# Longformer attention with a mixer behind it: two row groups for the global tokens' products, and the second token layer's last rows for two batches at once

## The chip, the cores and the metric

The kernel runs on one core of one Trainium2 chip. The metric is the time of one execution on the device, in microseconds, as the median of several runs. Beside the timed runs there is one execution under the hardware profiler; every row of a profile below comes from that one. In its rows PE is TensorE (PEld its weight loads), DVE is VectorE, ACT is ScalarE, POOL is GpSimd, and SP is the engine that issues most DMAs; a q behind an engine's name is its sequencer. L595 is line 595 of the kernel.

## The reference

Eight batches of eight heads, 576 tokens, 64 values a head. Attention sees a band of 32 tokens to each side, and eight global tokens, which see all and are seen by all. Its output, 576 x 512 for a batch, goes through a mixer: a token layer over the 576 tokens and a channel layer over the 512 channels, each with a relu in the middle and a residual.

```python
mask = |i - j| <= 32  or  i is global  or  j is global
attn = softmax(where(mask, q @ k.T / 8, -1e9))
x = (attn @ v)                                  # (8, 576, 512), heads side by side
h = relu(x.T @ w_tok1) @ w_tok2                 # w_tok1 (576, 256), w_tok2 (256, 576)
u = x + h.T
out = u + relu(u @ w_ch1) @ w_ch2               # w_ch1 (512, 1536), w_ch2 (1536, 512)
```

## The kernel before

**Tiling.** The 576 tokens are four tiles of 128 and a last one of 64. Matrix products take 16-bit floats and add up in 32-bit in TensorE's output memory, from which VectorE or ScalarE fetch the results. Three pools hold these outputs: `psS`, three buffers of two times 512 columns, for attention and the token layers; `psM`, two of 512 columns, for the channel layers.

**Steps of a batch.** `S_` computes transposed scores of a pair of heads, each head on 64 of the array's 128 rows (`r = slice(64 * par, 64 * par + 64)`), ScalarE takes their exponentials into `e_all`, and `SM` masks them. `GK` computes the scores of the global keys, for four pairs of heads in four groups of 32 output rows, and gives `lf`: on row 32 p + 16 r + g stands head 2 p + r, and g counts eight global keys (the other eight rows of the sixteen are masked). `OG` sums the values that belong to these rows; its result, multiplied with a block pattern `blk`, is `rf`. `PV` (from L576) makes one tile of 128 tokens of x: for each head two products of 66 columns from the band (L586, L591; the last tile has one), and then for each half of four heads one product of `lf` with `rf` over all 128 rows and 264 columns (L595), which adds the global keys. VectorE divides by the sums and writes the tile into `x16s` (L602, L603).

**Token layers.** `M1` multiplies a tile of x with `w1` (two products of 512 columns for each tile, L618); after the fifth tile the relu gives `a1`. The fifth tile has 64 tokens. An even batch keeps them on rows 0 to 63 of its tile, an odd batch on rows 64 to 127; the weights for it, `w1l`, exist in two copies with the other rows at zero. `M2(b, part)` is the second token layer: parts 0 and 1 make two tiles of 128 tokens each (four products of 512 columns, L642, with adds on VectorE, L648), part 2 the last 64 tokens (two products and an add on 64 rows, L651). An even and the following odd batch share one tile `ul` for these, so that the channel layers of the last rows (`M4l`, the last `M5`) run once for two batches. `M3` transposes u by DMA on SP's queue, for the channel layers. Batch 0 has versions of its own (`M23_first`, `M3_first`), where TensorE transposes.

**Channel layers.** `M4` (twelve steps of four products, L697, with a relu on ScalarE, L703) and `M5` (eight steps of six products, L726, with an add and a store) are independent of the next batch's attention. They stand in a list, `dense`.

**Order.** The order of each engine's queue is written by hand: an instruction stands in the queue of its engine in the order in which the program calls it. `period(b)` runs the dense list of batch b between the attention steps of batch n = b + 1; `d(k)` takes the next k entries. In the same period the loads, casts and transposes of q and k for batch n + 1 and beyond are called (m = b + 2). `casts(b, engine)` lists nine casts of one batch: the rest rows first, then q and k of each pair of heads. For batch 3 the period n = 2 calls three of them on ScalarE behind `scores(0, ..)`, two behind `scores(1, ..)`, and the last three on Pool, then issues batch 4's loads on Pool (`load(4)`) and batch 3's transposes on SP (`turns(3)`).

**Loads.** Ahead of batch 0's value products Pool issues the weights, mixed with casts of v (`castv`): `w1`; then both copies of `w1l` and `w2` (`load_wt`, L223); then the channel weights, the gathers of the global tokens, and half of batch 1's q and k. SP loads the first batches' q, k and v and, later, those of batch 3.

Of the kernel before, what the change touches and what calls it, by code (L numbers as in the profile page):

```python
# [26 lines left out]
def kernel(  # L27
# [142 lines left out]
    idx_i = const.tile([P, 4], I32)  # L170
    gpm = const.tile([P, 1], F32)
    hb = const.tile([P, 1], F32)
    blk = const.tile([P, H], F32)

    def positions():
        nc.vector.tensor_mul(out=sel, in0=sel, in1=gidx_f)
# [36 lines left out]

    w1 = const.tile([P, NT - 1, DTOK], F16)
    w1l = const.tile([P, 2, DTOK], F16)
    w2 = const.tile([P, 2, NT * P], F16)
    wc1 = const.tile([P, 4, DCH], F16)
    wc2 = const.tile([P, NJ, DM], F16)

    def load_w1():  # L220
        nc.gpsimd.dma_start(out=w1, in_=moe_w_tok1[0 : S - LAST, :].rearrange("(c p) x -> p c x", p=P))

    def load_wt():  # L223
        nc.gpsimd.dma_start(out=w1l[0:LAST, 0], in_=moe_w_tok1[S - LAST : S, :])
        nc.gpsimd.dma_start(out=w1l[LAST:P, 1], in_=moe_w_tok1[S - LAST : S, :])
        nc.gpsimd.dma_start(out=w2[:, :, 0:S], in_=moe_w_tok2.rearrange("(c p) x -> p c x", p=P))

    def load_wc1(h0):
        nc.gpsimd.dma_start(
# [17 lines left out]
    nc.gpsimd.memset(kgz, 0.0)  # L247

    eg = const.tile([P, NT, H, GW], F16)
    x16s = [const.tile([P, NT, DM], F16, name=f"x16_{i}") for i in range(2)]  # L250

    def w_pads():
        nc.gpsimd.memset(w1l, 0.0)
        nc.gpsimd.memset(w2[:, :, S:], 0.0)

    def pads(i, eng):
        eng.memset(vsh[i][0:WIN, 0], 0.0)
        eng.memset(vsh[i][P - WIN : P, NT - 1], 0.0)
        eng.memset(vsh[i][:, :, :, D + 1 : VW], 0.0)
        eng.memset(vsh[i][:, :, :, D : D + 1], 1.0)  # L260
        eng.memset(x16s[i][LAST - 64 * i : P - 64 * i, NT - 1, :], 0.0)

    far = const.tile([P, NT, EW - 64], F16)
    bandm = const.tile([P, NT, EW - 64], F16)
# [295 lines left out]
    def OG(b):  # L560
        s = st[b]
        ps = pss([P, 2, VW], name=f"og_{b}")
        for c in range(NT):
            for p in range(NP):
                nc.tensor.matmul(  # L565
                    ps[32 * p : 32 * p + 32], lhsT=eg[:, c, 2 * p : 2 * p + 2, :],
                    rhs=vsh[b % 2][:, c, 2 * p : 2 * p + 2, :], start=(c == 0), stop=(c == NT - 1),
                )
        rf = mb.tile([P, NP, 2, VW], F16, tag="rf", name=f"rf_{b}")
        nc.vector.tensor_tensor(  # L570
            out=rf, in0=ps.unsqueeze(1).to_broadcast([P, NP, 2, VW]),
            in1=blk.rearrange("p (n r) -> p n r", r=2).unsqueeze(3).to_broadcast([P, NP, 2, VW]), op=ALU.mult,
        )
        s["rf"] = rf

    def PV(b, tau):  # L576
        s = st[b]

        odd_last = tau == NT - 1 and b % 2 == 1
        sh = 64 if odd_last else 0  # L580
        ps = pss([P, 2, 512], name=f"pv_{b}_{tau}")
        for hf in range(2):
            for hh in range(NP):
                h = NP * hf + hh
                o = ps[:, hf, VW * hh : VW * hh + VW]
                nc.tensor.matmul(  # L586
                    o, lhsT=e_all[:, h, tau, EW - P - sh : EW - sh], rhs=vsh[b % 2][:, tau, h, :],
                    start=hh == 0, stop=False,
                )
                if tau < NT - 1:  # L590
                    nc.tensor.matmul(  # L591
                        o, lhsT=e_all[:, h, tau + 1, 0:P], rhs=vsh[b % 2][:, tau + 1, h, :], start=False, stop=False
                    )
        for hf in range(2):
            nc.tensor.matmul(  # L595
                ps[:, hf, 0 : NP * VW], lhsT=s["lf"][:, P * tau - sh : P * tau - sh + P],
                rhs=s["rf"][:, 2 * hf : 2 * hf + 2], start=False, stop=True,
            )
# [4 lines left out]
        nc.vector.tensor_tensor(  # L603
            out=x16s[b % 2][r, tau, :].rearrange("p (f h x) -> p f h x", f=2, h=NP), in0=pq[r, :, :, 0:D],
            in1=rr[r].unsqueeze(3).to_broadcast([P if tau < NT - 1 else 64, 2, NP, D]), op=ALU.mult,
        )

    def M1(b, ch):
        s = st[b]
        if ch == 0 and b == 0:  # L610
            s["a1p"] = [psm([P, 512], name=f"a1p_{b}_{tt}") for tt in range(2)]
        elif ch == 0:
            ps = pss([P, 2, 512], name=f"a1p_{b}")
            s["a1p"], s["a1pp"] = [ps[:, 0], ps[:, 1]], ps
        ps = s["a1p"]
        for tt in range(2):
            w = w1[:, ch, P * tt : P * tt + P] if ch < NT - 1 else w1l[:, b % 2, P * tt : P * tt + P]
            nc.tensor.matmul(ps[tt], lhsT=w, rhs=x16s[b % 2][:, ch, :], start=(ch == 0), stop=(ch == NT - 1))  # L618
# [10 lines left out]
        if b % 2 == 0:  # L629
            s["ul"] = mb.tile([P, DM], F16, tag="ul", name=f"ul_{b}")  # L630
        else:
            s["ul"] = st[b - 1]["ul"]

    def M2(b, part):
        s = st[b]
        x16 = x16s[b % 2]
        taus = ((0, 1), (2, 3), (4,))[part]
        ps = pss([P, 2, 512], name=f"hp_{b}_{part}")
        sh = 64 if (part == 2 and b % 2) else 0
        for i, tau in enumerate(taus):  # L640
            for ch in range(2):
                nc.tensor.matmul(  # L642
                    ps[:, i, :], lhsT=w2[:, ch, P * tau - sh : P * tau - sh + P], rhs=s["a1"][:, ch, :],
                    start=(ch == 0), stop=(ch == 1),
                )
        if part < 2:
            for i, tau in enumerate(taus):
                nc.vector.tensor_add(out=s["u16"][:, tau], in0=x16[:, tau], in1=ps[:, i])  # L648
        else:
            r = slice(sh, sh + 64)  # L650
# [104 lines left out]
    def period(b):  # L755
# [30 lines left out]
        if n == 1:  # L786
            d(1)
            gather_t(0)
            globals_(1)
            T(1, 1)  # L790
            TE_q(1, 1, act)
            TE_k(1, 1, dve)
            masks_d()
            pads(1, nc.vector)
            d(1)
# [173 lines left out]
    load_wc1(8)  # L969
    load_wc2(0)  # L970
    load_wc2(4)
    GK(0)
    OG(0)
    lf_mask(0, 384)
# [61 lines left out]
```

## Time and profile before

| | us |
|---|---|
| three timed runs: median | 313.42 |
| lowest and highest | 313.31 to 315.36 |
| profiled execution | 313.69 |
| its span, from the first to the last instruction | 311.9 |

The granted clock of TensorE was 0.997 of the full one over the span. The chain that ended last, followed back from the last instruction, lies on TensorE for 82% of the span and on DMAs for 7%; 29% are the second channel layer (L726), 25% the first (L697). In lists by line a row reads: line, engine, operation, what it writes and reads, sizes, count, then busy time and the mean of one. In timelines the first column is the start in us from the beginning of the span, the second the time from the first start to the last end of the instructions in that row; what stands in brackets is idle time ahead of them, and what ended it.

### The profile page before, as it was taken

The numbers are of one execution on the slowest core, as the hardware profiler recorded it, in microseconds if no ns is written. First come the engines' busy times: TensorE is split into PE (matmuls) and PEld (weight loads), VectorE is DVE, ScalarE is ACT, GpSimd is POOL, SyncE is SP. The second block draws the span as 40 slices with busy tenths as digits, with TensorE's granted clock in tenths as the row PEclk, the third lists the DMA queues.
The fourth block names the chain that finished last, engine by engine and source line by source line (L and its number), as shares of the span: only waits on it lengthen the run. The fifth ranks groups of instructions, "written<-read, shape, count | busy, mean of one in ns | idle before, by whom it ended". The sixth has DMA issues, their size and how long they took to land.

```text
span 311.9 us, 6688 instructions
## 1 busy us (share of the span) xinstructions
PE 297.4 (95%) x2672; PEld 158.4 (51%) x2672; DVE 193.1 (62%) x429; ACT 164.2 (53%) x289; POOL 75.0 (24%) x118
## 2 busy tenths in 40 slices
PE   8987989997999999999999999999999999999993
PEld 7563545453465445544574445544574446444641
DVE  7985797575655677577854577577744585530021
ACT  5864773466739465576548473676443283206500
POOL 8785960496622002300230003200000000000000
PEclk9999999999999999999999999999999999999998
DMA  6999999899999999948995699954602410051022
GB/s 195 234 250 223 224 181 286 234 244 193 241 202 155 176 358 143 106 84 260 261 129 55 164 355 119 98 124 139 95 20 50 138 49 2 12 138 71 0 103 67
DMA packets 108513, 48.19 MB, mean 154 GB/s; under 512 B 87106, under 2 KB 102338, under 8 KB 108482
## 3 DMA queue, kind: packets, MB, share of 16 engines
q1 hardware_dynamic: 69712, 33.83, 48.3%
q0 software_dynamic: 38768, 13.93, 36.5%
q8 instruction: 21, 0.34, 0.5%
q14 instruction: 10, 0.08, 0.1%
q10 hardware_dynamic: 2, 0.00, 0.0%
HBM read 36.11 MB, written 9.44 MB: 146 GB/s over the span
## 4 chain that ended last, share of the span: by engine, by line
PE 82%; DMA 7%; DVE 3%; ACT 2%; SPq 2%; POOL 1%; issue 1%
PE op L726 29%; PE b1p L697 25%; PE hp L642 5%; PE a1p L618 5%; PE s L474 4%; PE b1lp L713 3%; DMA w<-in_moe_w_tok_dram 3%; PE pv L586 3%; PE pv L595 3%; DMA lv<-in_v_dram 2%; PE pv L591 2%; DMA uT<-u 2%; SPq L86 1%; PE og L565 1%; DVE e_all L538 1%
## 5 line engine op out<-in xcount | busy, mean ns | idle before, releaser
L697 PE MATMUL b1p<-uT,wc 128*128 128x512 f16 x384 | 94.3, 380 | 3.0 <-DMA uT<-u 1.5
L726 PE MATMUL op<-wc,b 128*128 128x512 f16 x384 | 88.1, 379 | 0.0
L703 ACT ACTIVATE b<-b1p 128x512 f16<-128x512 f32 x87 | 52.7, 606 | 63.0 <-PE b1p L697 59.8
L726 PEld LDWEIGHTS <-b 128*128 128x128 f16 x384 | 36.4, 98 | 43.4 <-ACT b L703 0.2
L697 PEld LDWEIGHTS <-wc 128*128 128x128 f16 x384 | 35.1, 98 | 44.8 <-issue 6.7
L360 POOL DMA_DIRECT2D vsh<-in_v_dram x35 | 30.5, 882 | 98.2 <-PE pv L595 90.5
L730 DVE TENSOR_TENSOR osb<-u,op 128x512 f32<-128x512 f16 x32 | 22.0, 686 | 46.7 <-PE op L726 46.6
L494 ACT ACTIVATE e_all<-s 128x832 f16<-128x832 f32 x32 | 27.8, 868 | 40.3 <-issue 27.1
L538 DVE TENSOR_TENSOR e_all<-e_all,bandm 128x1040 f16<-128x1040 f16 x56 | 37.3, 706 | 1.0
L648 DVE TENSOR_TENSOR u<-x,hp 128x512 f16<-128x512 f16 x28 | 17.4, 682 | 23.1 <-PE hp L642 23.1
L603 DVE TENSOR_TENSOR x<-pv,rr 128x512 f16<-128x512 f32 (+1 forms) x40 | 27.6, 691 | 1.4
L586 PEld LDWEIGHTS <-e_all 128*128 128x128 f16 x320 | 20.9, 97 | 5.5 <-DVE x L603 0.5
L586 PE MATMUL pv<-vsh,e_all 128*128 128x66 f16 x320 | 23.1, 193 | 0.0
L511 ACT ACTIVATE e_all<-s 128x576 f16<-128x576 f32 x32 | 21.0, 656 | 0.5 <-PE s L474 0.5
L474 PE MATMUL s<-qT,kT 64*128 64x208 f16 (+1 forms) x320 | 19.2, 241 | 1.0 <-ACT e_all L494 1.0
L591 PE MATMUL pv<-vsh,e_all 128*128 128x66 f16 x256 | 19.8, 193 | 0.0
L602 DVE RECIPROCAL rr<-pv 128x8 f32<-128x8 f32 (+1 forms) x40 | 8.3, 206 | 18.5 <-PE pv L595 18.2
L371 ACT CAST qk<-lq 128x512 f16<-128x512 f32 x28 | 16.9, 617 | 3.7 <-DMA lq<-in_q_dram 3.7
L474 PEld LDWEIGHTS <-kT 64*128 64x128 f16 x320 | 11.1, 94 | 15.2 <-issue 13.1
L618 PE MATMUL a1p<-x,w 128*128 128x512 f16 x64 | 18.7, 379 | 0.0
L591 PEld LDWEIGHTS <-e_all 128*128 128x128 f16 x256 | 16.6, 97 | 3.0
L516 ACT ACTIVATE e_all<-s 128x416 f16<-128x416 f32 x32 | 17.2, 536 | 0.0
(181 smaller groups left out, 345.9 us busy)
## 6 DMA issues: line engine op xcount, KB each, us to landing
out_dram<-osb SPq DMA_DIRECT2D x32, 256.0 KB, 2.6
lq<-in_q_dram SPq DMA_DIRECT2D x4, 1024.0 KB, 6.4
lk<-in_k_dram SPq DMA_DIRECT2D x4, 1024.0 KB, 8.6
wc<-in_moe_w_ch_dram POOLq DMA_DIRECT2D x6, 512.0 KB, 9.8
vsh<-in_v_dram POOLq DMA_DIRECT2D x21, 128.0 KB, 7.7
lq<-in_q_dram POOLq DMA_DIRECT2D x2, 1024.0 KB, 9.9
lk<-in_k_dram POOLq DMA_DIRECT2D x2, 1024.0 KB, 12.9
vsh<-in_v_dram POOLq DMA_DIRECT2D x14, 96.0 KB, 7.2
```

Of the source, the lines that this page charges most:

```text
L360: nc.gpsimd.dma_start(out=vsh[b % 2][r0:r1, c, :, 0:D], in_=v[b, :, j0 : j0 + (r1 - r0), :].rearrange("h p d -> p h d"),)
L474: nc.tensor.matmul(ps[:, par, off : off + n], lhsT=kT[r, P * c : P * c + P], rhs=qf[r, lo : lo + n], start=b > 0, stop=b > 0 or c > 1 and ...
L494: nc.scalar.activation(out=e2[:, :, 1:3, 64:EW], in_=ps[:, :, 0 : 2 * W].rearrange("p h (c x) -> p h c x", c=2), func=AF.Exp, scale=scale,)
L538: nc.vector.tensor_mul(out=eh, in0=eh, in1=bandm)
L586: nc.tensor.matmul(o, lhsT=e_all[:, h, tau, EW - P - sh : EW - sh], rhs=vsh[b % 2][:, tau, h, :], start=hh == 0, stop=False,)
L591: nc.tensor.matmul(o, lhsT=e_all[:, h, tau + 1, 0:P], rhs=vsh[b % 2][:, tau + 1, h, :], start=False, stop=False)
L603: nc.vector.tensor_tensor(out=x16s[b % 2][r, tau, :].rearrange("p (f h x) -> p f h x", f=2, h=NP), in0=pq[r, :, :, 0:D], in1=rr[r].unsquee ...
L618: nc.tensor.matmul(ps[tt], lhsT=w, rhs=x16s[b % 2][:, ch, :], start=(ch == 0), stop=(ch == NT - 1))
L697: nc.tensor.matmul(ps, lhsT=wc1[:, cc, P * j : P * j + P], rhs=s["uT"][:, cc, :], start=(cc == 0), stop=(cc == 3))
L703: nc.scalar.activation(out=s["b1"][:, j, :], in_=ps, func=AF.Relu)
L726: nc.tensor.matmul(ps, lhsT=w, rhs=wc2[:, j, :], start=(j == 0), stop=(j == NJ - 1))
L730: nc.vector.tensor_add(out=osb, in0=s["u16"][:, tau], in1=ps)
```

## The change

- `rf` has for each row only the two pairs of heads of its half (264 columns in place of 528), and `blk` four columns in place of eight. The two products of L595 take rows 0 to 63 (first four heads) and rows 64 to 127 (last four), each with its own half of `lf` and `rf`.
- The last 64 tokens of both batches of a pair live in one tile, `xl`. Part 2 of `M2` goes; `M2l`, called in odd batches, makes the last rows of both batches in one output tile, the even batch's on rows 0 to 63, the odd one's on rows 64 to 127, with one add on VectorE. `a1` has two buffers, since the even batch's is read a period later. The call `M2(0, 2)` among batch 1's scores goes.
- `w2` is loaded right behind `w1`, ahead of the casts of v; `w1l` is loaded in two calls, its second copy behind the channel weights. The zero columns of `w2` go, and with them a memset.
- Batch 3's casts of q and k are called on Pool, all eight behind `GK(2)`.
- In period n = 1 one `d(1)` stands ahead of `masks_d` and `pads(1, ..)` instead of behind.

```diff
-        h4 = int_op("h4", 4, ALU.logical_shift_right)
-        nc.vector.tensor_copy(out=blk, in_=cc_i)
+        h4 = int_op("h4", 4, ALU.logical_shift_right, 3, ALU.bitwise_and)
+        nc.vector.tensor_copy(out=blk, in_=cc_i[:, 0:NP])
...
-        rf = mb.tile([P, NP, 2, VW], F16, tag="rf", name=f"rf_{b}")
+        rf = mb.tile([P, 2, 2, VW], F16, tag="rf", name=f"rf_{b}")
...
         for hf in range(2):
+            rows = slice(64 * hf, 64 * hf + 64)
             nc.tensor.matmul(
-                ps[:, hf, 0 : NP * VW], lhsT=s["lf"][:, P * tau - sh : P * tau - sh + P],
-                rhs=s["rf"][:, 2 * hf : 2 * hf + 2], start=False, stop=True,
+                ps[:, hf, 0 : NP * VW], lhsT=s["lf"][rows, P * tau - sh : P * tau - sh + P],
+                rhs=s["rf"][rows], start=False, stop=True,
             )
...
-        a1 = mb.tile([P, 2, DM], F16, tag="a1", bufs=1, name=f"a1_{b}")
+        a1 = mb.tile([P, 2, DM], F16, tag="a1", name=f"a1_{b}")
...
-            nc.vector.tensor_add(out=s["ul"][r], in0=x16[r, NT - 1], in1=ps[r, 0])
+    def M2l(b):
+        ps = pss([P, 512], name=f"hpl_{b}")
+        for ch in range(2):
+            for i in range(2):
+                nc.tensor.matmul(
+                    ps[64 * i : 64 * i + 64], lhsT=w2[:, ch, P * (NT - 1) : S], rhs=st[b - 1 + i]["a1"][:, ch, :],
+                    start=(ch == 0), stop=(ch == 1),
+                )
+        st[b]["ul"] = mb.tile([P, DM], F16, tag="ul", name=f"ul_{b}")
+        nc.vector.tensor_add(out=st[b]["ul"], in0=xl, in1=ps)
...
-        if n == 1:
-            M2(0, 2)
-        if n == 2:
-            c3 = casts(3, nc.scalar.copy)
-            for c in c3[1:4]:
-                c()
         scores(1, max(tail - 4 - (tail > 5), 0))
-        if n == 2:
-            for c in c3[4:6]:
-                c()
-            for c in casts(3, nc.gpsimd.tensor_copy)[6:]:
-                c()
         scores(2, 0)
         GK(n)
...
         if n == 2:
+            for c in casts(3, nc.gpsimd.tensor_copy)[1:]:
+                c()
             load(4)
             turns(3)
...
-        M2(n, 2)
         if n % 2:
+            M2l(n)
             M3(n, 2)
...
     load_w1()
+    load_w2()
     castv(0, (1, 2, 3))
-    load_wt()
+    load_w1l(0)
     load_wc1(0)
...
     load_wc2(4)
+    load_w1l(1)
     GK(0)
```

More of the change, by code (lines that the diff above doesn't have):

```diff
@@ L172 @@
     hb = const.tile([P, 1], F32)
-    blk = const.tile([P, H], F32)
+    blk = const.tile([P, NP], F32)
     def positions():
@@ L215 @@
     w1l = const.tile([P, 2, DTOK], F16)
-    w2 = const.tile([P, 2, NT * P], F16)
+    w2 = const.tile([P, 2, S], F16)
     wc1 = const.tile([P, 4, DCH], F16)
@@ L221, in load_w1, with load_w1l, load_w2 @@
         nc.gpsimd.dma_start(out=w1, in_=moe_w_tok1[0 : S - LAST, :].rearrange("(c p) x -> p c x", p=P))
[L223 to L226, printed above, removed]
+    def load_w1l(i):
+        nc.gpsimd.dma_start(out=w1l[LAST * i : LAST * i + LAST, i], in_=moe_w_tok1[S - LAST : S, :])
+    def load_w2():
+        nc.gpsimd.dma_start(out=w2, in_=moe_w_tok2.rearrange("(c p) x -> p c x", p=P))
     def load_wc1(h0):
@@ L249, with x_of @@
     eg = const.tile([P, NT, H, GW], F16)
-    x16s = [const.tile([P, NT, DM], F16, name=f"x16_{i}") for i in range(2)]
+    x16s = [const.tile([P, NT - 1, DM], F16, name=f"x16_{i}") for i in range(2)]
+    xl = const.tile([P, DM], F16)
+    def x_of(b, tau):
+        return x16s[b % 2][:, tau, :] if tau < NT - 1 else xl
     def w_pads():
         nc.gpsimd.memset(w1l, 0.0)
-        nc.gpsimd.memset(w2[:, :, S:], 0.0)
     def pads(i, eng):
@@ L260, in pads @@
         eng.memset(vsh[i][:, :, :, D : D + 1], 1.0)
[L261 removed]
+        if i == 0:
+            eng.memset(xl[LAST:P], 0.0)
     far = const.tile([P, NT, EW - 64], F16)
@@ L603, in PV @@
         nc.vector.tensor_tensor(
-            out=x16s[b % 2][r, tau, :].rearrange("p (f h x) -> p f h x", f=2, h=NP), in0=pq[r, :, :, 0:D],
+            out=x_of(b, tau)[r].rearrange("p (f h x) -> p f h x", f=2, h=NP), in0=pq[r, :, :, 0:D],
             in1=rr[r].unsqueeze(3).to_broadcast([P if tau < NT - 1 else 64, 2, NP, D]), op=ALU.mult,
@@ L628, in M1 @@
         s["u16"] = mb.tile([P, 4, DM], F16, tag="u16", name=f"u16_{b}")
[L629 to L632, printed above, removed]
     def M2(b, part):
         s = st[b]
-        x16 = x16s[b % 2]
-        taus = ((0, 1), (2, 3), (4,))[part]
         ps = pss([P, 2, 512], name=f"hp_{b}_{part}")
-        sh = 64 if (part == 2 and b % 2) else 0
-        for i, tau in enumerate(taus):
+        for i, tau in enumerate((2 * part, 2 * part + 1)):
             for ch in range(2):
                 nc.tensor.matmul(
-                    ps[:, i, :], lhsT=w2[:, ch, P * tau - sh : P * tau - sh + P], rhs=s["a1"][:, ch, :],
+                    ps[:, i, :], lhsT=w2[:, ch, P * tau : P * tau + P], rhs=s["a1"][:, ch, :],
                     start=(ch == 0), stop=(ch == 1),
                 )
[L646 to L650, printed above, removed]
-            nc.vector.tensor_add(out=s["ul"][r], in0=x16[r, NT - 1], in1=ps[r, 0])
+        for i, tau in enumerate((2 * part, 2 * part + 1)):
+            nc.vector.tensor_add(out=s["u16"][:, tau], in0=x_of(b, tau), in1=ps[:, i])
+    def M2l(b):
[8 more added lines that the diff above has]
+        nc.vector.tensor_add(out=st[b]["ul"], in0=xl, in1=ps)
     def M23_first(tau):
```

8 lines of the change are left out of this document (4 added, 4 removed).

## The prediction

> **What bounds the kernel now.** I read the page first, for the engines' shares, then the windows by stage, TensorE's waits, and last the timelines of the places that the diff touches. The page gives TensorE nearly the whole span:
>
> ```profile
> PE 297.4 (95%) x2672; PEld 158.4 (51%) x2672; DVE 193.1 (62%) x429; ACT 164.2 (53%) x289; POOL 75.0 (24%) x118
> ```
>
> The windows (busy us of each engine in each stretch, then clock, DMA share, GB/s) say where this average hides other limits, and the list of TensorE's waits names them:
>
> ```profile
> core 0: us, PE busy (x) PEld busy (x) DVE busy (x) ACT busy (x) POOL busy (x), PEclk, DMA share, GB/s
> 14.00:56.00 42.00, 37.43 (x455) 21.73 (x452) 33.75 (x87) 25.81 (x48) 25.69 (x37) 1.00 1.23 234
> 56.00:73.00 17.00, 15.67 (x113) 8.05 (x111) 12.40 (x23) 8.56 (x15) 13.08 (x18) 1.00 1.13 210
> 73.00:83.00 10.00, 8.54 (x77) 3.71 (x78) 4.79 (x11) 8.52 (x17) 7.09 (x9) 1.00 1.49 220
> 83.00:280.00 197.00, 197.00 (x1679) 102.33 (x1680) 126.28 (x253) 102.97 (x182) 17.75 (x20) 1.00 0.83 140
> ```
>
> ```profile
> PE hp L659 <- DMA w<-in_moe_w_tok_dram: 2.0, 1, 2.0
> PE b1p L697 <- DMA uT<-u: 1.5, 1, 1.5
> PE b1p L697 <- ACT b L703: 1.3, 2, 0.8
> ```
>
> So there are three regimes. From 83 to 280 us TensorE is busy 197.00 of 197.00 us: every nanosecond added to or taken from its queue there goes into the time one for one. Up to 73 us the DMA engines are oversubscribed (share 1.23, then 1.13) and TensorE waits for two transfers. From 73 to 83 us it waits for ScalarE. I add up each regime by itself.
>
> **The value products of the global tokens (L595), two row groups of 64.** Before, each PV has two 128-row products of 264 columns behind sixteen short ones:
>
> ```profile
> 189.72 0.19 PE L591 MATMUL pv<-vsh,e_all 128*128 128x66 f16 x1
> 189.75 0.39 PE L595 MATMUL pv<-rf,lf 128*128 128x264 f16 x2
> 189.97 1.03 PE L697 MATMUL b1p<-uT,wc 128*128 128x512 f16 x4
> ```
>
> An instruction's duration overlaps the next one's start here, so the cost in the queue is from start to start: 189.97 - 189.75 = 0.22 us for the two, 0.11 each. The rate is the same for long products:
>
> ```profile
> 200.39 2.32 PE L642 MATMUL hp<-a,w 128*128 128x512 f16 x10
> 202.54 0.81 PE L726 MATMUL op<-wc,b 128*128 128x512 f16 x3
> ```
>
> Ten of 512 columns take 202.54 - 200.39 = 2.15, 0.215 each or 0.42 ns a column. After, each half uses 64 rows of the array, as the scores do already:
>
> ```profile
> 212.60 0.38 PE L726 MATMUL op<-wc,b 128*128 128x512 f16 x1
> 212.91 0.57 PE L474 MATMUL s<-qT,kT 64*128 64x208 f16 x10
> ```
>
> ```profile
> 213.23 0.25 PE L474 MATMUL s<-qT,kT 64*128 64x208 f16 x2
> 213.41 0.82 PE L697 MATMUL b1p<-uT,wc 128*128 128x512 f16 x3
> ```
>
> The last two score products both start at 213.23: row groups do run at once. But look at the edges. The 512-column product at 212.60 holds the queue for 0.215 us, so the scores could start at 212.82 and start at 212.91: 0.09 lost. The last pair streams 208 columns, 0.09 us at the same rate, so the product behind it could start at 213.32 and starts at 213.41: 0.09 again. Each change between the full array and half arrays leaves TensorE's queue empty for 0.09 to 0.095 us, in and out. In PV the pair stands alone between full-array products on both sides (L591 before, M1 or a dense product behind), so every pair pays both. Per PV: 0.11 for both halves at once, plus 2 x 0.095, is 0.30, against 0.22: **+0.08 us**. The bounds are -0.11 (no edge is paid) and +0.19 (edges paid, halves one after the other); I take +0.08, because the score rows show both effects in the same form of instruction. The Trainium skill (TensorEngine Tiling (Array Packing), Tiling Modes, Key Properties) says that a change of the tiling mode, not of the tile alone, drains TensorE; the trace agrees, with the 0.09 at either edge. By that rule the sum is the one below, by overlap alone the first rival's.
>
> Of 40 PVs, 30 (batches 2 to 7) lie behind 73 us: 30 x 0.08 = **+2.4 us**. rf halves from 528 to 264 columns on VectorE, which is not the limit from 83 us on.
>
> **The last rows of the second token layer, two batches at once.** Before, each batch issues two 512-column products for them (the row of ten above has eight for the rest): 4 x 0.215 = 0.86 us for a pair of batches. After, only the odd batch issues four, each 64 columns wide in weights, two at a time in two column groups. Column groups are in the trace at L565, four at once:
>
> ```profile
> 187.67 0.38 PE L697 MATMUL b1p<-uT,wc 128*128 128x512 f16 x1
> 187.98 0.47 PE L565 MATMUL og<-vsh,eg 128*32 128x132 f16 x20
> 188.39 1.04 PE L697 MATMUL b1p<-uT,wc 128*128 128x512 f16 x4
> ```
>
> Twenty products of 132 columns would take 1.11 us one after the other, 0.28 four at a time. From 187.67 + 0.215 = 187.89 to 188.39 are 0.50: overlap, plus 0.22 at the edges. So M2l costs 2 x 0.215 + 0.20 = 0.63, a gain of 0.86 - 0.63 = 0.23 us per pair; bounds +0.43 (no edge) and -0.20 (no overlap). For the three pairs behind 73 us: 3 x 0.23 = **-0.7 us**. The adds saved on VectorE are off the path there. The double buffer of a1 adds no wait: its first half is free once the pair before is done, a period earlier.
>
> **Batch 3's casts from ScalarE to Pool.** Behind these two casts ScalarE's queue is the one that TensorE waits for, twice:
>
> ```profile
> 74.76 0.61 ACT L371 CAST qk<-lk 128x512 f16<-128x512 f32 x1
> 75.27 0.62 ACT L371 CAST qk<-lq 128x512 f16<-128x512 f32 x1
> 75.79 0.87 ACT L494 ACTIVATE e_all<-s 128x832 f16<-128x832 f32 x1
> ```
>
> ```profile
> 77.73 1.02 PE L697 MATMUL b1p<-uT,wc 128*128 128x512 f16 x4 [0.82 <-ACT b L703]
> ...
> 81.56 1.02 PE L697 MATMUL b1p<-uT,wc 128*128 128x512 f16 x4 [0.47 <-ACT b L703]
> ```
>
> Two of the five casts leave this stretch, 75.79 - 74.76 = 1.03 us. The first wait goes whole (0.82), of the second some 0.3 is left by the same bookkeeping (relu, exps and relu in their order): **-1.1 us**, bounds -1.3 (both waits) and 0 (the wait moves to another engine). The other three casts stood before 73 us, in idle time. Pool takes eight casts in place of three. They cannot start before the row
>
> ```profile
> 70.31 0.69 POOL L371 CAST qk<-lk 128x512 f16<-128x512 f32 x1
> ```
>
> and five more of 0.69 end 3.5 us later than the three did. That is the most by which the queues behind them are late: on Pool batch 4's loads (four issues), on SP batch 3's nine transposes and what follows these. Batch 3's scores, which need them, stand a period later (197 us / 6 = 33), so the cost is nothing as long as that cover holds; without it, it is the 3.5.
>
> **w2 sooner, and everything else before 73 us.** The first wait of the list is at the start:
>
> ```profile
> 14.54 0.99 POOL L221 DMA_DIRECT2D w<-in_moe_w_tok_dram  x1
> 15.58 1.78 POOL L411 CAST vsh<-lv 128x512 f16<-128x512 f32 x3
> 17.30 0.56 POOL L224 DMA_DIRECT2D w1l<-in_moe_w_tok_dram  x1
> 17.85 0.53 POOL L225 DMA_DIRECT2D w1l<-in_moe_w_tok_dram  x1
> 18.37 0.74 POOL L226 DMA_DIRECT2D w<-in_moe_w_tok_dram  x1
> ```
>
> ```profile
> 25.55 0.59 PE L618 MATMUL a1p<-x,w1l 128*128 128x512 f16 x2
> 28.09 1.04 PE L659 MATMUL hp<-a,w 128*128 128x512 f16 x4 [1.95 <-DMA w<-in_moe_w_tok_dram]
> ```
>
> w2 is issued at about 15.5 instead of 18.4, and the step at 28.09 could start up to 1.95 us sooner. Against that, w1l's first half now stands behind w2 in Pool's DMA queue and is needed at 25.55; its second half goes to the end of the weights. One add of VectorE and M2(0, 2) leave the scores of batch 1 (two products, 0.43), and batches 0 and 1 pay ten PVs (+0.8) and an M2l. I cost the lot at nothing, because the next transfer wait takes it up:
>
> ```profile
> 58.25 2.28 POOL L371 CAST qk<-lk 128x512 f16<-128x512 f32 x4 [11.45 <-DMA lk<-in_k_dram]
> ```
>
> ```profile
> 60.56 0.37 SPq L86 DMA_DIRECT2D lk<-in_k_dram  x1
> 61.02 0.53 SPq L731 DMA_DIRECT2D out_dram<-osb  x1
> 61.65 5.79 SPq L684 DMA_TRANSPOSE uT<-u  x4
> ```
>
> ```profile
> 73.16 1.02 PE L697 MATMUL b1p<-uT,wc 128*128 128x512 f16 x4 [1.46 <-DMA uT<-u]
> ```
>
> Pool waits 11.45 us for batch 2's k; its casts end at 60.53; only then can SP load batch 3's k (60.56) into the same buffer, and batch 1's transposes queue behind that load. TensorE's 73.16 hangs on bytes that the change does not reduce. Work before it that ends sooner makes the 1.46 longer, work that ends later (up to 1.46) makes it shorter. Bounds: -1.5 (the transposes do not queue, and the wait goes) and +1.0 (an early delay of 2.5 outlasts the 1.46).
>
> **Sum.** On the profiled run's 313.69 us (span 311.9, 1.8 around it): +2.4 - 0.7 - 1.1 + 0 = +0.6. The median of the runs shown, 313.42, is 0.27 lower; on it the forecast is **314.0 us**.
>
> **Rivals.**
> 1. *Grouping for nothing.* If no edge is paid, each PV gains 0.11 (30 x 0.11 = 3.3), each pair 0.43 (1.3), ScalarE's 1.1 stays: 5.7 less, 307.7 us. For it: 213.23, two products at once. Against it: the 0.09 at both edges of every such group in the timelines above. The Trainium skill (same page, Theoretical Speedup) promises up to 2x where a dimension is at most 64; here K is 128 before and is cut in two, so its best case is this rival. Chance 0.13.
> 2. *Half the edge.* Short products 0.03 us apart stand before the pair; if the change into half arrays overlaps with their tail, and is not paid, 30 x 0.095 = 2.85 less: 311.2 us. The trace has no such neighbour of a pair from 83 us on. Chance 0.10.
> 3. *It does not do what it says (the slower end).* The halves drain the array but run one after the other, as they accumulate onto products of the full array: 30 x 0.11 = 3.3 more, 317.3 us. It decides once the second half starts 0.1 us behind the first. Against it: the scores' pairs, each half into its own 512 columns as here. Chance 0.07.
> 4. *Early loads turn against it.* w1l lands behind w2 as late as w2 does now (28.09), and M1's last step slips by 28.09 - 25.55 = 2.5. The 1.46 holds its part, 1.0 comes on top: 315.0; where the loads behind it slip too, the whole: 316.5. Against it: w1l is small, and w2 ahead of it is issued 2.8 sooner. Chance 0.12.
>
> My forecast has the remaining 0.58; its own range is 313.2 to 315.0. The range 310.8 to 316.4 holds it with rivals 2 and 4 (0.80). One per cent, about what a measurement here can tell, is 3.1 us: faster is rival 1 (0.13), slower rival 3 (0.07), the rest is within.
>
> **What would show it.** In the timeline after: two L595 starts at one time, some 0.12 us behind the last short product, and 0.2 to the next; if the pair takes 0.11 from edge to edge, rival 1. TensorE still 100% busy from 83 us to 32 us before the end, that stretch longer by some 1.7 us. M2l: four products in about 0.63 us. The wait for w2 gone, the one for uT at about 73.2 still there and not at another time by over 1 us; if that start moves, my absorption is wrong. The waits for ScalarE at 77.7 and 81.6 down by about 1 us.

## The result, and the profile after

The changed kernel took 316.39 us (median of 17 executions, 315.05 to 319.12), the kernel before, between them, 314.11 us: a ratio of 1.0073, 95% interval 1.0056 to 1.0090. On another chip, timed again in the last experiment, it was 1.0046 (1.0016 to 1.0076). A ratio leaves out executions over 1.5% longer than the fastest of the same kernel (six of twelve of fill_short, five of act_early_again, two of act_early, at most one of any other), while the counts of executions with a low clock, further down, take them in. The profiled execution took 316.37 us against 313.69, its span is 314.2 us against 311.9. In the changed kernel the lines are L592 and L597 for the band's products (L586, L591 before), L602 for the row groups (L595), L609 and L610 for the divisions, L654 for M2l, L705 for M4, L734 for M5.

The windows of the changed kernel, columns as in the prediction:

```profile
14.00:56.00 42.00, 36.68 (x411) 20.22 (x408) 30.96 (x79) 26.19 (x50) 25.01 (x36) 0.96 1.24 237
56.00:73.00 17.00, 17.00 (x138) 8.73 (x138) 11.96 (x21) 5.23 (x9) 12.78 (x18) 1.00 0.97 202
73.00:83.00 10.00, 9.42 (x88) 4.31 (x87) 8.28 (x16) 8.60 (x17) 10.00 (x13) 1.00 1.32 236
83.00:280.00 197.00, 197.00 (x1669) 98.84 (x1667) 121.48 (x249) 103.02 (x182) 18.19 (x22) 1.00 0.84 136
```

From 83 us on nothing has changed in kind: TensorE is full. From 56 to 73 us it is now full too (15.67 before), and in the first window it lost some clock (0.96). The list of its waits says what became of the two transfers:

```profile
PE pv L592 <- issue: 1.5, 2, 1.1
...
PE pv L602 <- issue: 0.6, 1, 0.6
PE b1p L705 <- DVE b L709: 0.6, 1, 0.6
...
PE b1p L705 <- DVE osb L738: 0.4, 1, 0.4
PE pv L597 <- issue: 0.4, 1, 0.4
PE b1p L705 <- ACT b L711: 0.3, 1, 0.3
```

The waits for w2 and uT are gone. New are the 2.5 us of "issue" ahead of value products, in which the profile shows nothing that TensorE waited for. The waits for b, 0.6 us for VectorE and 0.3 us for ScalarE, lie between 45 and 56 us, in batch 0's channel layer. From 73 to 83 us two waits are left: 0.43 us for VectorE's osb at 75.79 us, and 0.14 us for ScalarE at 81.5 us, too short for this list.

Where the time went is read best from two marks that every variant has: the first product of b(1), batch 1's first channel layer (73.16 us before), and OG of batch 2. The rows of OG and of the last twelve products of M5, first the kernel before:

```profile
82.52 0.47 PE L565 MATMUL og<-vsh,eg 128*32 128x132 f16 x20
304.14 2.75 PE L726 MATMUL op<-wc,b1l 128*128 128x512 f16 x12
```

then the changed kernel, with b(1) ahead:

```profile
73.83 1.03 PE L705 MATMUL b1p<-uT,wc 128*128 128x512 f16 x4
82.47 0.47 PE L571 MATMUL og<-vsh,eg 128*32 128x132 f16 x20
306.50 2.75 PE L734 MATMUL op<-wc,b1l 128*128 128x512 f16 x12
```

Behind OG it is 224.03 us against 221.62, 2.41 more. From b(1) to OG it is 8.64 against 9.36, 0.72 less. b(1) itself starts 0.67 later. These three make 2.36 of the 2.68 us between the profiled executions; most of the rest lies outside the span (2.17 against 1.79 us).

### The profile page after: what moved, and what is told of

Read it like the earlier page. It is cut to its first block, busy times and chain, and to the rows that moved or that the text cites. A ratio compares the mean times of both kernels' runs of the same rounds, so it can differ in the third digit from the quotient of the medians.

```text
span 314.2 us, 6679 instructions
## 1 busy us (share of the span) xinstructions
PE 301.4 (96%) x2672; PEld 156.1 (50%) x2672; DVE 189.7 (60%) x424; ACT 161.8 (51%) x284; POOL 77.8 (25%) x122
## 4 chain that ended last, share of the span: by engine, by line
PE 86%; DVE 10%; ACT 1%; issue 1%
PE op L734 29%; PE b1p L705 25%; PE a1p L625 7%; PE hp L642 4%; PE s L480 4%; PE pv L592 3%; PE b1lp L721 3%; PE pv L602 3%; PE pv L597 3%; DVE e_all L544 2%; DVE qT L449 1%; DVE kT L455 1%; PE og L571 1%; PE idle L893 1%; PE hpl L654 1%
## 5 line engine op out<-in xcount | busy, mean ns | idle before, releaser
L705 PE MATMUL b1p<-uT,wc 128*128 128x512 f16 x384 | 94.5, 380 | 1.4 <-DVE b L709 0.6
L734 PE MATMUL op<-wc,b 128*128 128x512 f16 x384 | 88.1, 379 | 0.0
L734 PEld LDWEIGHTS <-b 128*128 128x128 f16 x384 | 36.0, 98 | 44.1 <-issue 1.6
L705 PEld LDWEIGHTS <-wc 128*128 128x128 f16 x384 | 34.6, 98 | 43.7 <-issue 5.0
L592 PE MATMUL pv<-vsh,e_all 128*128 128x66 f16 x320 | 24.1, 196 | 1.5 <-issue 1.5
L592 PEld LDWEIGHTS <-e_all 128*128 128x128 f16 x320 | 21.4, 99 | 7.7 <-issue 2.3
L609 DVE RECIPROCAL rr<-pv 128x8 f32<-128x8 f32 (+1 forms) x40 | 8.3, 206 | 27.3 <-PE pv L602 26.4
L610 DVE TENSOR_TENSOR x<-pv,rr 128x512 f16<-128x512 f32 x32 | 22.1, 691 | 1.1
L597 PE MATMUL pv<-vsh,e_all 128*128 128x66 f16 x256 | 20.6, 194 | 0.4 <-issue 0.4
L625 PE MATMUL a1p<-x,w 128*128 128x512 f16 x64 | 19.7, 395 | 0.0
L597 PEld LDWEIGHTS <-e_all 128*128 128x128 f16 x256 | 17.1, 98 | 3.5 <-issue 0.5
L377 ACT CAST qk<-lq 128x512 f16<-128x512 f32 x25 | 15.2, 622 | 6.6 <-DMA lq<-in_q_dram 6.6
```

Of the source, the lines that this page charges most:

```text
L592: nc.tensor.matmul(o, lhsT=e_all[:, h, tau, EW - P - sh : EW - sh], rhs=vsh[b % 2][:, tau, h, :], start=hh == 0, stop=False,)
L597: nc.tensor.matmul(o, lhsT=e_all[:, h, tau + 1, 0:P], rhs=vsh[b % 2][:, tau + 1, h, :], start=False, stop=False)
L610: nc.vector.tensor_tensor(out=x_of(b, tau)[r].rearrange("p (f h x) -> p f h x", f=2, h=NP), in0=pq[r, :, :, 0:D], in1=rr[r].unsqueeze(3).t ...
L625: nc.tensor.matmul(ps[tt], lhsT=w, rhs=x_of(b, ch), start=(ch == 0), stop=(ch == NT - 1))
L705: nc.tensor.matmul(ps, lhsT=wc1[:, cc, P * j : P * j + P], rhs=s["uT"][:, cc, :], start=(cc == 0), stop=(cc == 3))
L734: nc.tensor.matmul(ps, lhsT=w, rhs=wc2[:, j, :], start=(j == 0), stop=(j == NJ - 1))
```

## The experiments

Each ratio is against the kernel before on the same chip, with its 95% interval, from 9 to 13 executions of the kernel named (groups_only: six).

| kernel | what it is | ratio |
|---|---|---|
| groups_only, groups_again | before + row groups | 1.0118 (1.0073 to 1.0163), 1.0092 (1.0058 to 1.0127) |
| groups_paired | the same, two tiles' groups side by side | 1.0013 (0.9991 to 1.0035) |
| no_groups | after without row groups | 0.9962 (0.9931 to 0.9993) |
| casts_only | before + batch 3's casts on Pool | 0.9956 (0.9929 to 0.9984) |
| m2l_only | before + M2l and xl, with the moved d(1) | 0.9983 (0.9958 to 1.0009) |
| m2l_casts | before + M2l, xl and the casts | 1.0001 (0.9972 to 1.0031) |
| act_early, again | before + M2l, two casts earlier on ScalarE | 0.9974 (0.9950 to 0.9999), 0.9974 (0.9941 to 1.0007) |
| order_only | before + new places of w2 and w1l | 1.0010 (0.9983 to 1.0037) |
| old_order | after with the old places | 1.0089 (1.0055 to 1.0122) |
| act_early_order | act_early + new places | 0.9947 (0.9909 to 0.9985) |
| act_early_fill | act_early + 64 products of zeros | 0.9987 (0.9962 to 1.0011) |
| fill_short | act_early + 40 products of zeros | 0.9979 (0.9940 to 1.0018) |
| after_timed | the changed kernel | 1.0046 (1.0016 to 1.0076) |

**The row groups.** groups_only and groups_again are the kernel before with `blk`, `rf` and the products of the diff above; no_groups is the changed kernel with these lines, and those of `rf` and `blk`, as before:

```diff
-            rows = slice(64 * hf, 64 * hf + 64)
...
-                ps[:, hf, 0 : NP * VW], lhsT=s["lf"][rows, P * tau - sh : P * tau - sh + P],
-                rhs=s["rf"][rows], start=False, stop=True,
+                ps[:, hf, 0 : NP * VW], lhsT=s["lf"][:, P * tau - sh : P * tau - sh + P],
+                rhs=s["rf"][:, 2 * hf : 2 * hf + 2], start=False, stop=True,
```

> The kernel before with the two row groups alone. Edge theory: 30 x 0.09 = 2.7 us more behind 83 us, and what the first two batches pay (0.9) is taken up by the wait for uT at 73 us, which shrinks from 1.46; so 1.0086 of before. Rival, no absorption: 3.6 us more, 1.0115. Rival, edges free: 3.3 us less. No stall at batch 0's third tile.

> The changed kernel with the global products back on all 128 rows; all else as changed. Edge theory (each change between full and half arrays costs 0.095 us, 0.09 us more per value-product tile): 30 tiles behind 83 us give back 2.7 us against the changed kernel, so some 313.5 us or 0.997 of the kernel before, and two L595-like products start 0.11 us apart. Grouping for nothing: the time rises by 3.3 us against the changed kernel. The early stall of the changed kernel (third tile of batch 0, some 3 us) stays, if the order of the loads makes it.

The groups cost what all else in the change gives back, and more. The visit in the timeline of the changed kernel:

```profile
190.52 0.20 PE L592 MATMUL pv<-vsh,e_all 128*128 128x66 f16 x1
190.55 0.19 PE L597 MATMUL pv<-vsh,e_all 128*128 128x66 f16 x1
190.67 0.29 PE L602 MATMUL pv<-rf,lf 64*128 64x264 f16 x2
190.89 1.04 PE L705 MATMUL b1p<-uT,wc 128*128 128x512 f16 x4
```

Short products are 0.03 apart, but the pair starts 0.12 behind the last one: 0.09 at the way in. The two halves share one row and take 0.22 to the next product, where 264 columns stream in 0.11: 0.11 at the way out. From the last short product to the dense one it is 0.34 against 0.25 before (189.72 to 189.97), and the first dense product behind takes 0.01 more (1.04 us for the four against 1.03): 0.10 in all.

groups_paired issues the pair of the next tile right behind the first one's, ahead of that tile's band products, for two couples of tiles in each batch from batch 2 on; so TensorE changes over three times a batch, not five.

```diff
+        ahead = b > 1 and tau in (1, 3)
...
+        if not ahead:
+            PV_pair(b, tau, False)
+        if b > 1 and tau in (0, 2):
+            PV_pair(b, tau + 1, True)
```

> As groups_only, but in batches 2 to 7 the row groups' products of tiles 0 and 1, and of 2 and 3, stand together: three visits to half arrays a batch in place of five. The sums are the same. Edge theory (0.2 us for each visit): 6 batches x 2 visits x 0.2 = 2.4 us less than groups_only, 1.004 of before. If the half-array products themselves were slow, and not the edges: as groups_only, 1.012.

It came out at 1.0013, far below groups_only and less even than expected. Its timeline shows why:

```profile
189.45 0.19 PE L608 MATMUL pv<-vsh,e_all 128*128 128x66 f16 x1
189.57 0.40 PE L584 MATMUL pv<-rf,lf 64*128 64x264 f16 x4
189.91 1.04 PE L713 MATMUL b1p<-uT,wc 128*128 128x512 f16 x4
```

Four products instead of two, and the same 0.12 ahead; behind them 0.34, 0.12 more for the second pair, which is its streaming time and no edge. From OG of batch 2 on it is 222.69 us, of which 0.60 are a wait for v in the middle of OG; without these it is 0.47 more than before, where the 3.02 of all groups (below) less 0.2 for each of twelve couples would make 0.62. So it is the change-over that costs, not the half array. groups_again gives the size, with more executions:

> The row groups alone on the kernel before, as in groups_only, with more executions. 30 groups behind 73 us at +0.10 us each make +3.0 us: 1.0095 (1.008 to 1.011). If the +3.5 us of the six executions before is right, 1.011 or more, and a further 0.5 us comes from elsewhere.

```profile
81.35 0.47 PE L565 MATMUL og<-vsh,eg 128*32 128x132 f16 x20
305.99 2.75 PE L727 MATMUL op<-wc,b1l 128*128 128x512 f16 x12
```

From OG on 224.64 us against 221.62: +3.02 us for the 30 groups, 0.10 each. By the times it was 1.0092, 2.9 us of 313.0.

**M2l and the casts.** casts_only takes the eight casts to Pool in the kernel before, m2l_only takes `M2l`, `xl`, two buffers of `a1` and the moved `d(1)` with the old casts and loads, m2l_casts both:

```diff
-            c3 = casts(3, nc.scalar.copy)
-            for c in c3[1:4]:
-                c()
...
+            for c in casts(3, nc.gpsimd.tensor_copy)[1:]:
+                c()
             load(4)
```

> The kernel before with batch 3's eight casts on Pool behind GK(2), nothing else. My first price: ScalarE's two waits go, 1.1 us less (0.9965). Theory from the first four traces: while Pool casts, VectorE's masks hardly move (a pair takes 3 us and more in place of 1.3 to 1.9), TensorE waits for VectorE in place of ScalarE, and batch 4's transposes come later, so that VectorE waits for them in batch 3's value products; so between 1.000 and 1.006, OG of batch 2 no sooner than 82.0 us.

> The kernel before with the second token layer's last rows for two batches at once, nothing else. Edge theory: an even batch loses two products (0.43 us), an odd one pays 0.65 in place of 0.43; three pairs behind 83 us: 0.65 us less (0.998). If the wait of about 1 us ahead of batch 3's last token-layer step, seen in the two runs without row groups, comes from the casts on Pool, it is not here; if from the shared tile of last rows, it is.

> The changed kernel without row groups and with the old order of loads: what is left is the second token layer for two batches at once and batch 3's casts on Pool. Edge theory: -0.65 us from the former behind 83 us (three pairs, 0.86 against 0.65), -1.1 from the casts between 73 and 83 us: 1.75 less, 0.9945 of before. If Pool's casts delay something instead: not under 0.998.

casts_only, from b(1) to OG:

```profile
72.69 1.02 PE L697 MATMUL b1p<-uT,wc 128*128 128x512 f16 x4 [1.43 <-DMA uT<-u]
...
80.08 1.02 PE L697 MATMUL b1p<-uT,wc 128*128 128x512 f16 x4 [0.33 <-ACT b L703]
81.03 0.47 PE L565 MATMUL og<-vsh,eg 128*32 128x132 f16 x20
```

8.34 us, 1.02 less than before, and of the two waits for ScalarE 0.33 is left. Its expectation's dearer forecast, 1.000 to 1.006, missed: masks beside the casts are slow here too (3.28 us for a pair), but the add for osb behind them came in time for TensorE. m2l_only, from OG on:

```profile
81.88 0.47 PE L571 MATMUL og<-vsh,eg 128*32 128x132 f16 x20
302.88 2.75 PE L733 MATMUL op<-wc,b1l 128*128 128x512 f16 x12
```

221.00 us against 221.62: -0.62. With the groups' +3.02 that makes +2.40, where the changed kernel has +2.41: behind OG the two edits add up. Together in m2l_casts, however, M2l and the casts brought nothing by the times, where 0.9945 was expected. Three things stand out in its profile. Pool's casts hold VectorE, here two masks from 67.80 us on that took 1.31 us in other places; TensorE was waiting for uT by then, and no wait for VectorE follows up to OG:

```profile
67.80 5.27 DVE L544 TENSOR_TENSOR e_all<-e_all,bandm 128x1040 f16<-128x1040 f16 x2
...
75.05 1.31 DVE L544 TENSOR_TENSOR e_all<-e_all,bandm 128x1040 f16<-128x1040 f16 x2
```

TensorE reaches b(1) early, waits longer for uT, and then runs at half the clock (windows of TensorE alone: busy time, clock, DMA share, GB/s):

```profile
72.20 1.02 PE L704 MATMUL b1p<-uT,wc 128*128 128x512 f16 x4 [2.42 <-DMA uT<-u]
```

```profile
72.00:74.00 2.00, 1.80 (x15) 0.95 1.87 209
74.00:76.00 2.00, 2.00 (x6) 0.50 1.80 239
76.00:78.00 2.00, 2.00 (x13) 0.70 1.22 305
```

And at 130 us TensorE waits 0.97 us for `xl`. no_groups, which has the same two changes, shows what is behind such a wait: VectorE stands until a transpose of batch 4's q and k has landed, and the division for `xl` comes after it.

```profile
127.86 0.68 DVE L398 COPY kT<-raw 128x512 f16<-128x512 f16 x1 [1.25 <-DMA raw<-qk]
129.57 0.59 PE L624 MATMUL a1p<-xl,w1l 128*128 128x512 f16 x2 [0.86 <-DVE xl L609]
```

casts_only and m2l_only have no wait behind OG, so neither edit makes it alone. It is the cover of which the prediction says that the cost is nothing as long as it holds; the changed kernel has no such wait.

act_early leaves Pool out: m2l_only with the two casts that stood behind `scores(1, ..)` a step earlier, in the middle of these scores, still on ScalarE.

```diff
+            if n == 2 and p == 1:
+                for c in casts(3, nc.scalar.copy)[4:6]:
+                    c()
```

> As m2l_only, and two of ScalarE's casts of batch 3 stand one step sooner, ahead of the relu of batch 1's first channel step instead of behind it, where ScalarE is idle for 2.8 us. If ScalarE's queue set the pace from 73 to 83 us: OG of batch 2 1.0 us sooner than before (81.5), the masks undisturbed, and 1.65 us less in all (0.995). If batch 4's transposes then hold VectorE near 122 and 128 us: only 0.65 less (0.998). If the early casts gain nothing: OG at 82.5.

From b(1) to OG it takes 8.34 us, as in casts_only: the two casts only had to leave the place where TensorE waits for ScalarE.

**The places of the loads.** old_order is the changed kernel with w2 and w1l as before, order_only the kernel before with the new places, act_early_order act_early with them.

```diff
     load_w1()
+    load_w2()
     castv(0, (1, 2, 3))
-    load_wt()
+    load_w1l(0)
...
     load_wc2(4)
+    load_w1l(1)
```

> The changed kernel with the loads of w1l and w2 in their old order. If the new order makes the early stall, it goes: batch 0's second token layer starts near 28.1 us as before (30.7 in the changed kernel), batch 1's channel layer at 73.2 (73.8 in the changed kernel), the waits for ScalarE at 77 and 81 us shrink by 1.1, and the whole is +2.0 - 1.1 = 0.9 us above before (1.003). If the order does not matter: 1.007 as the changed kernel, with the stall.

> The kernel before with the new places of the w2 and w1l loads alone. Forecast: TensorE's wait for w2 goes, nothing comes of it, as the wait for uT takes it up: b(1) starts at 72.1 to 73.2 us and the time is 0.998 to 1.002 of the kernel before. The rival, that the new order itself stalls TensorE at the value products of batch 0 at 21 to 25 us: a stall there of over 1 us with no releaser, and 1.000 to 1.005.

> Paired last rows and early ScalarE casts (act_early), with the new places of the w2 and w1l loads besides. Between them the two orders differed in one thing so far: with the new one 1 of 12 executions showed a granted clock below 0.996, with the old one 7 or 8 of 12, as TensorE gets to the wait for uT sooner there. If the order does that, dips are few here (at most 3 of 12) and the ratio is 0.993 to 0.995; if the number of dips has another cause, some 7 of 12 and 0.997 as in act_early.

Alone the new places bring nothing (1.0010). old_order, at neither of the two forecasts, and act_early_order lean to a gain of about 0.2%, within their intervals. The closest pair is m2l_casts and no_groups, on one chip, which differ in nothing else: 1.0001 and 0.9962, with intervals that overlap. The expected drop in executions with a low clock did not come: act_early_order has 8 of 12. What goes with the new places in most profiles is a loss of TensorE at 21 to 25 us. VectorE's rows there, in the changed kernel:

```profile
23.33 0.21 DVE L609 RECIPROCAL rr<-pv 128x8 f32<-128x8 f32 x1 [2.37 <-PE pv L602]
23.57 0.69 DVE L610 TENSOR_TENSOR x<-pv,rr 128x512 f16<-128x512 f32 x1
24.90 0.21 DVE L609 RECIPROCAL rr<-pv 128x8 f32<-128x8 f32 x1 [0.64 <-remote]
```

The product that the first is said to wait for had started at 20.81 us. VectorE stands until 23.3 us, and TensorE, in the middle of the next tile, works from 21.95 to 24.73 us only in snatches (gaps of 0.39, 0.43 and 1.14 us), while Pool issues the four gathers of the global tokens (19.01 to 23.86 us); TensorE's clock is half for a while behind that. Is it the kernel or that one execution?

> The changed kernel, not altered, profiled a second time. If the 1.5 us that TensorE lost at 21.95 to 24.73 us, with no releaser that the profile shows, belong to the kernel, they are seen again at the value products of batch 0, its second token layer starts at 30 us or later again and the TensorE clock falls to half behind it; if they belong to that one execution, the second token layer starts at 26 to 28 us as in the variants so far, b(1) starts at 72.1 to 73.2 us, and the profiled time is nearer to 315.6 us. I expect the second (0.6).

The second profile of the same kernel (315.68 us) has it again, until 25.0 us, against the expectation; the third (after_timed) has not, though its gathers stand at the same time (18.98 to 23.84 us): its second token layer starts at 27.07 us, not 30.72 or 30.13. Of the six profiles with the new places four have it, of the twelve with the old ones one (act_early_fill). What sets it off was not found.

**The clock.** Beside m2l_casts, old_order showed the half clock behind a wait for uT (2.33 us). act_early, with a wait of 2.18, did not, and neither did m2l_only, with the longest wait for uT of all (its row, and its window of all engines from 72 to 77 us, clock 1.00):

```profile
72.55 1.02 PE L704 MATMUL b1p<-uT,wc 128*128 128x512 f16 x4 [2.18 <-DMA uT<-u]
```

```profile
72.52 1.02 PE L704 MATMUL b1p<-uT,wc 128*128 128x512 f16 x4 [2.45 <-DMA uT<-u]
72.00:77.00 5.00, 3.75 (x30) 1.60 (x31) 1.04 (x2) 3.37 (x7) 1.70 (x3) 1.00 1.49 245
```

Yet 7 of act_early's 12 timed executions had a mean granted clock below 0.996 (10 of 35 of the kernel before on that chip), and these were 2.1 us slower in the median. act_early_fill and fill_short (40 products) give TensorE work inside that wait:

```diff
+        if b == 1 and j == 0:
+            for _ in range(64):
+                nc.tensor.matmul(ps[:, 0:64], lhsT=wz, rhs=wz[:, 0:64], start=True, stop=True)
```

> act_early with 64 products of 64 columns from the zero weights put ahead of the first product of b(1), in its own bank, which the real products then overwrite: some 1.8 us of work for TensorE inside its wait of 2.2 us for uT (the order of w2 as in the kernel before). If TensorE's idling there is what makes the clock fall to half in 7 of 12 executions, the dips go (at most 3 of 12), the median falls to the 311.6 us of act_early's executions at full clock, and the ratio is 0.993 to 0.995; if the dips come from something else, they stay at some 7 of 12 and 0.997.

> act_early once more, as the partner of fill_short on this chip: 0.996 to 0.998, and TensorE's granted clock below 0.996 in about half of the executions.

> act_early with 40 instead of 64 products of zeros ahead of b(1): some 1.15 us by the 29 ns that one took, inside a wait of 2.2 us, so the product behind it isn't delayed. If idling ahead of b(1) lowers the clock, fewer executions than act_early_again's have a clock below 0.996 (at most 3 of 12) and the ratio is 0.002 to 0.004 below its; if not, the share and the ratio are the same within 0.002.

In the profile of act_early_fill, which has the early loss too, the last of uT's transposes had landed before the 64 products began (66.4 + 5.3 = 71.7 against 72.72 us), so they only delayed b(1), to 74.58 us; it can't answer the question. The 40 can: 0.27 us of the wait was left. Still 7 of 12 executions were below 0.996, as in act_early_again on the same chip (12 of 32 of the kernel before), and the ratios are the same. So the wait for uT is not what lowers the clock in most of them. The profiles of two of the low ones name other waits. In act_early_again OG of batch 2 waits for v:

```profile
84.06 0.30 PE L571 MATMUL og<-vsh,eg 128*32 128x132 f16 x4 [4.21 <-DMA vsh<-in_v_dram]
```

```profile
82.00:84.00 2.00, 0.00 (x0) 0.00 (x0) 0.00 (x0) 0.00 (x0) 0.00 (x0) 0.86 0.98 242
84.00:86.00 2.00, 1.95 (x9) 0.72 (x9) 0.71 (x1) 0.00 (x0) 1.55 (x2) 0.50 1.13 337
86.00:88.00 2.00, 2.00 (x25) 1.50 (x24) 0.68 (x2) 0.60 (x1) 0.82 (x2) 0.79 1.30 176
```

and in act_early_fill a product of M1 waits 2.35 us for x at 128 us, with the clock at 0.50 and 0.68 in the two windows of 2 us behind it. A kernel that gets to its transfers sooner, without their landing sooner, can thus pay twice: the wait, and the slow clock behind it. How often, these counts do not settle.

**The whole again.** What was left open after these was how much of the miss the groups carry.

> The changed kernel itself, on the chip of the others. If the casts and the paired last rows give what they give alone (about 0.8 and 0.75 us), the ratio is 1.3 to 1.8 us below that of groups_again: 1.004 to 1.006. If the early part of the kernel loses what the casts should give, it is only 0.7 us below: 1.007 to 1.008.

1.0046 against groups_again's 1.0092 on the same chip: 1.4 us less, so M2l and the casts gave most of what they give alone, as far as these intervals tell. Its marks are 71.96, 80.60 and 304.62 us: again 8.64 from b(1) to OG, and 224.02 behind it.

## Why the prediction was right in its sign and wrong in its size

The forecast was 0.6 us more; the two series say 2.3 and 1.4 us.

**Row groups, the term of the sum that failed by most: "30 x 0.08 = +2.4 us".** The mechanism held: two starts at one time, 0.12 behind the last short product, 0.22 to the next. The size did not: 0.10 for each PV, +3.0 us. The 0.09 at the way in was right; the way out costs 0.11, with 0.01 more in the product behind it, and the edges had been read off pairs of scores, at the second digit of the rows, where 0.02 in 0.08 is a quarter of the term.

**M2l, "-0.7 us"**, measured -0.62. In the changed kernel:

```profile
201.72 1.89 PE L642 MATMUL hp<-a,w 128*128 128x512 f16 x8
203.54 0.62 PE L654 MATMUL hpl<-a,w 128*64 128x512 f16 x4
204.09 2.76 PE L734 MATMUL op<-wc,b 128*128 128x512 f16 x12
```

Eight products of 0.215 end at 203.44; to 204.09 are 0.65, where 0.63 was forecast.

**Casts, "-1.1 us"**: the two waits less the 0.3 left are 0.82 + 0.47 - 0.3 = 0.99, not 1.1. That was right for the casts alone (-1.02, with the 0.3 of the second wait left), and mis-sized in the changed kernel: -0.72 in all three profiles. The step overlooked that Pool's casts run beside VectorE's masks. The first and the last of the eight on Pool:

```profile
71.21 0.69 POOL L377 CAST qk<-lq 128x512 f16<-128x512 f32 x1
...
76.12 0.60 POOL L377 CAST qk<-lk 128x512 f16<-128x512 f32 x1
```

The masks on VectorE, beside them and once they are done, the add between them, and TensorE's wait for it:

```profile
71.75 1.35 DVE L538 TENSOR_TENSOR eg<-e_all,bandm 128x160 f16<-128x160 f16 x1
73.13 2.01 DVE L544 TENSOR_TENSOR e_all<-e_all,bandm 128x1040 f16<-128x1040 f16 x2
75.06 0.68 DVE L738 TENSOR_TENSOR osb<-u,op 128x512 f32<-128x512 f16 x1
...
76.86 0.23 DVE L538 TENSOR_TENSOR eg<-e_all,bandm 128x160 f16<-128x160 f16 x1
77.12 1.31 DVE L544 TENSOR_TENSOR e_all<-e_all,bandm 128x1040 f16<-128x1040 f16 x2
```

```profile
75.79 1.89 PE L705 MATMUL b1p<-uT,wc 128*128 128x512 f16 x8 [0.43 <-DVE osb L738]
```

Beside the casts they take 1.35 and 2.01 us, later 0.23 and 1.31. The add for osb stands behind them on VectorE, and TensorE waits for it. Against casts_only that wait is new, and the second one for ScalarE shrinks from 0.33 to 0.14. In no_groups the same eight casts gave nothing: 9.47 us from b(1) to OG, with 1.27 of wait for osb. What they are worth hangs on which masks they meet, and the bound "0 (the wait moves to another engine)" had the mechanism.

**Everything before 73 us, "I cost the lot at nothing, because the next transfer wait takes it up".** The size holds to about 1 us, either way, from one execution to the next, and that is in part luck, for the step failed: the sign that the prediction named, the wait for uT still there, is missing in all three profiles of the changed kernel. b(1) starts at 73.16 us before and at 73.83, 73.16 and 71.96 after, while the last of uT's transposes landed at 72.4, 72.0 and 70.9 us (start and time to landing in the trace; 73.0 before). So TensorE, full from 56 to 73 us, had become the later of the two, and nothing was left to take up a delay: b(1) came when TensorE's own work was done, in the two profiles with the early loss and in the one without.

**The rivals.** No edge, and half the edge, fall with the 0.12 and 0.22; serial halves with the one row of two starts; the loads turned against it, by a late w1l, with TensorE's list of waits, which has none for w1l. The interval of order_only (to 1.0037) does not exclude that rival's 1 us, and the early loss, which goes with the new places, came by another way than the one it names.

With the terms as measured, and the early part still at nothing, the sum is +3.0 - 0.6 - 0.7 + 0 = +1.7 us, 0.5% and not 0.2%; the two series gave 0.46 and 0.73%. The difference between these two is within their intervals; the early loss, in two of the three profiles, is a candidate for it that was not tried alone.

The fastest of these kernels, which the times do not tell apart, do without row groups: act_early_order, casts_only and no_groups, at 0.995 to 0.996, ahead of both kernels.

## What to carry to other kernels

Before splitting a product over row groups, count how often the array changes over, not how many products get shorter: here a change-over and back costs 0.20 us, the time of nearly two products of 264 columns, and even with two pairs side by side behind one change-over, for four tiles of five, there was no gain (1.0013). An edge that is multiplied by 30 should be read at more digits than the profile's rows have, or from a stage that holds many of them. And work moved to GpSimd is not free for VectorE: look what runs on VectorE in the same microseconds.

## What the runs showed of the hardware that was not expected

- **Waits well under 3 us can halve TensorE's clock, and need not.** Behind waits of 2.33 us (old_order), 2.35, 2.42 and 4.21 us the granted clock was 0.50 for a while, and so it was in the changed kernel behind gaps of 0.39, 0.43 and 1.14 us within 2.8; behind 2.18 us (act_early) and 2.45 us (m2l_only) it stayed at 1.00. So the length of the wait alone does not decide. In the three windows of m2l_casts above 2 x (0.05 + 0.50 + 0.30) = 1.7 us of clock are lost, 3.4 us at half, and windows of 2 us give the same 1.7 for the other four stretches. The Trainium skill (TensorE: Matmul & The Clock Gate, Why this matters for your kernels and What's actually happening) advises no gaps over some 3 us, and tells of a free-running window of about 3.4 us; the length of the slow stretch agrees, but the gap that sufficed here was shorter, and no run here shows where a window begins.
- **GpSimd's casts hold VectorE's products of two inputs** for several times their own duration: 5.27 us for two masks that take 1.31, and 1.35 us for one that takes 0.23. VectorE's copies out of TensorE's output memory kept their 0.68 us beside the casts (at 75.66 us in the changed kernel). The Trainium skill (GPSIMD Engine Reference, Specifications) says that the two engines share their interfaces to SBUF and contend where a VectorE instruction has two inputs there; the trace agrees.
- **VectorE stood for 2 to 3 us, and TensorE for 1 to 2 of them,** beside GpSimd's gathers in five of eighteen profiles, with "remote" (a releaser that the profile names no further) or "issue" as the only releaser in most of these rows. No run here shows why.
